# Turning q, k and the block mask by transposing DMAs in the later pairs of a fused attention and Fourier-MLP kernel

## The chip, the cores and the metric

The kernel runs on one core of one Trainium2 chip. The metric is the device time of one execution in microseconds (us), given as the median of several runs. TensorE (PE) multiplies matrices, VectorE (DVE), ScalarE (ACT) and GpSimd (POOL) work elementwise, and SyncE (SP) issues DMAs. PEld is TensorE's loading of weights, which overlaps the products.

## The reference, cut to what matters

Attention over q, k, v of shape (4 batches, 8 heads, 768 positions, 64), all float32. The keys form 12 blocks of 64. Each query may see its own block and the three blocks whose mean key has the largest product with it, below the diagonal:

```python
k_rep = k.reshape(B, H, n_blocks, block, D).mean(axis=3)
gate_scores = np.einsum('bhsd,bhnd->bhsn', q, k_rep)
gate_scores = np.where(causal, gate_scores, -1000000000.0)
top_idx = np.argsort(gate_scores, axis=-1)[..., -top_k:]
...
scores = scale * np.matmul(q, k.transpose(0, 1, 3, 2))
scores = np.where(mask, scores, -1000000000.0)
...
X = np.fft.fft(x, axis=1)
X = np.fft.fft(X, axis=2)
mixed = np.real(X).astype(np.float32)
u = x + mixed
un = (u - mu) / np.sqrt(var + 1e-06)
ch = np.maximum(un @ w_ch1, 0.0) @ w_ch2
return (u + ch).astype(np.float32)
```

Here x is the attention output of a batch, 768 positions by 512 (the heads side by side), and the MLP has 2048 hidden units.

## The kernel before, in words

Two heads of one batch form a pair; there are 16 pairs (0 to 15), four to a batch. For a pair, the main loop runs six steps of scores (`stage_S`: score products into `sc`, then one exponential on ACT into `ptl`) and, at fixed steps (`USUAL`), the rest of the work of this pair and of the two that follow:

- `load_qk`, `load_v`: q and k four pairs ahead, v two pairs ahead, on the sync queue, in float32 (`qn`, `kn`, `vn`).
- `stage_A`: TensorE transposes q and k (tile `tp`, twelve float32 transposes a pair). VectorE sums the keys of each block out of it (`kr`, L294). The turned k goes to `kI` in float16 (ACT, L313), the turned q to `qT`, and from there by POOL to `qg` (`cast_q`, L242).
- `stage_B`: the gate. Up to pair 7 it is a float32 product of `qT` with the block sums `kr24`. From pair 8 on (`SPLIT = 8`), q and the sums are each written as a high and a low float16 part (`qh`, `ql`, `krx`; L289, L290, L306, L307), and the product has 48 columns. VectorE takes the third largest (`mx`, L342) and writes a 0/1 mask `gmp`.
- `stage_C`: TensorE transposes the mask (`gt`, L356) and VectorE copies it into rows 64 to 75 of `qg` (L359). Those rows of `kI` hold -60000 at each block's own number, so the score product adds the mask.
- `stage_AV`: the product with v (`av`, L414). POOL casts v to float16 (`cast_v`, L237). Then the division and `fold`, which adds and subtracts halves for the Fourier transform; some small parts of it run on POOL (L443).

When a batch's four pairs are done, `queue_batch` puts its Fourier transform (`stage_S1`: `za`, `ya`; `stage_S2`: `mx`), its normalization (`stage_N`), the turning of the normalized x (`stage_T`: `unT`, by transposing DMAs for batches 1 and 2 and two parts of batch 3, L570) and its MLP (`stage_M1`: `ha`, `hb`; `stage_M2`: `ch`) into a feed. `filler` takes from the feed between the steps of the next pairs, by estimated costs and gaps, so that MLP products of the batch before stand between the score products. Batch 0's transform, in pairs 4 to 6, has no MLP work beside it.

The order on PE and POOL is the order of the program's text. On the other engines and the sync queue a scheduler chooses it. The MLP weights are loaded and cast to float16 by DMAs of POOL, each burst after a one-element copy that waits for a tile of a later pair (`pool_after`).

Of the kernel before, what the change touches and what calls it, by code (L numbers as in the profile page):

```python
# [19 lines left out]
def _consts_np():  # L20
    S = 768
    DM = 512
    NB = 12
    s = np.arange(S)

    sh = np.arange(S // 2)
    kk = 2 * np.arange(S // 4 + 1)[None, :] + np.arange(2)[:, None]
    arg = 2.0 * np.pi * ((sh[:, None, None] * kk[None]) % S) / S
    CS = np.cos(arg).astype(np.float16)
    SS = np.sin(arg).astype(np.float16)  # L30


    d = np.arange(DM // 4)
    l = 2 * np.arange(DM // 2)[None, :] + np.arange(2)[:, None]
    argd = 2.0 * np.pi * ((d[:, None, None] * l[None]) % DM) / DM
    CD = np.cos(argd).astype(np.float16)
    sn = np.sin(argd)
    sn[0] = np.sin(np.pi * l / 2)
    SDN, SDP = (-sn).astype(np.float16), sn.astype(np.float16)
    SDN[0, 0] = SDP[0, 0] = np.where(np.arange(DM // 2) % 2 == 0, 1.0, -1.0)  # L40
    ident32 = np.eye(128, dtype=np.float32)
    ident16 = np.eye(128, dtype=np.float16)
    jj = np.arange(128)
    ltri = np.where(jj[:, None] > jj[None, :], np.float32(NEG), 0.0).astype(np.float16)
    ut01 = (jj[:, None] <= jj[None, :]).astype(np.float16)
    nn = np.arange(NB)
    cz = np.where((s // 64)[:, None] >= nn[None, :], 0.0, -1e9).astype(np.float32)
    cz24 = np.concatenate([cz, cz], axis=1)
    oth01 = ((s // 64)[:, None] != nn[None, :]).astype(np.float16)
    oth24 = np.concatenate([oth01, oth01], axis=1)  # L50
    IndN = np.where(nn[:, None] == (s[None, :] // 64), NEG, 0.0).astype(np.float16)
    return dict(CS=CS, SS=SS, CD=CD, SDN=SDN, SDP=SDP, ident32=ident32, ident16=ident16,
                ut01=ut01, ltri=ltri, cz24=cz24, oth24=oth24, IndN=IndN)
# [65 lines left out]
def kernel(  # L119
# [65 lines left out]
    kI_t = [[const([128, S], F16, f"kI_{e}_{sl}") for sl in range(3)] for e in range(2)]  # L185
    v16_t = [const([128, 2, NST, 66], F16, f"v16_{sl}") for sl in range(4)]
    qg_t = [[const([128, S], F16, f"qg_{e}_{sl}") for sl in range(3)] for e in range(2)]
    warm = const([128, 512], F16, "warm")
    kr24_t = [const([128, 2 * NB], FP, f"kr24_{sl}") for sl in range(2)]
    krx_t = [const([128, 2, 2 * NB], F16, f"krx_{sl}") for sl in range(2)]  # L190
# [11 lines left out]
    SPLIT = 8  # L202
# [32 lines left out]
    def cast_v(kk):  # L235
        P[kk]["v16"] = v16_t[kk % 4]
        nc.gpsimd.tensor_copy(out=v16_t[kk % 4][:, :, :, 0:64], in_=P[kk]["vn"])  # L237

    def cast_q(kk):
        d = P[kk]  # L240
        for e in range(2):
            nc.gpsimd.tensor_copy(out=d["qg"][e][0:64, :],  # L242
                                  in_=d["qt" if kk < SPLIT else "qh"][64 * e:64 * e + 64, :])

# [21 lines left out]
    def stage_A(kk, who, g):  # L266
        d = P[kk]
        src = d["qn"] if who == 0 else d["kn"]
        if who == 0 and g == 0:
            d["qt"] = apool.tile([128, S], FP, tag="qT32", name=f"qT32_{kk}")  # L270
            if kk >= SPLIT:
                parts = d["qt"].bitcast(F16)
                d["qh"], d["ql"] = parts[:, 0:S], parts[:, S:2 * S]
            d["qg"] = [qg_t[e][kk % 3] for e in range(2)]
        if who == 1 and g == 0:
            d["kI"] = [kI_t[e][kk % 3] for e in range(2)]
            d["kr12"] = spool.tile([128, NB], FP, tag="kr12", name=f"kr12_{kk}", bufs=2)
            d["kr24"] = kr24_t[kk % 2]
        ps = pst([128, 3, 128], f"tp_{kk}_{who}_{g}")
        for i in range(3):  # L280
            nc.tensor.transpose(ps[:, i, :],  # L281
                                src[:, 3 * g + i, :, :].rearrange("p h d -> p (h d)"), id32)
        flat = ps.rearrange("p a c -> p (a c)")
        cols = slice(384 * g, 384 * (g + 1))
        if who == 0:
            if kk < SPLIT:
                (nc.scalar.copy if kk == LATE else nc.vector.tensor_copy)(out=d["qt"][:, cols], in_=flat)
            else:
                nc.scalar.activation(out=d["qh"][:, cols], in_=flat, func=AF.Copy, scale=QS)  # L289
                STT(out=d["ql"][:, cols], in0=flat, scalar=QS, in1=d["qh"][:, cols], op0=MULT, op1=SUB)  # L290
            if g == 1 and kk != LATE:
                cast_q(kk)
        else:
            nc.vector.tensor_reduce(out=d["kr12"][:, 6 * g:6 * g + 6],  # L294
                                    in_=ps.rearrange("p a (x c) -> p a x c", x=2),
                                    axis=mybir.AxisListType.X, op=ADD)
            if g == 1 and kk < SPLIT:
                for e in range(2):
                    nc.vector.tensor_copy(out=d["kr24"][64 * e:64 * e + 64, NB * e:NB * (e + 1)],
                                          in_=d["kr12"][64 * e:64 * e + 64, :])  # L300
            elif g == 1:
                d["krx"] = krx_t[kk % 2]
                for e in range(2):
                    r, c = slice(64 * e, 64 * e + 64), slice(NB * e, NB * (e + 1))
                    hi, lo = d["krx"][r, 0, c], d["krx"][r, 1, c]
                    nc.vector.tensor_scalar(out=hi, in0=d["kr12"][r, :], scalar1=QS, scalar2=None, op0=MULT)  # L306
                    STT(out=lo, in0=d["kr12"][r, :], scalar=QS, in1=hi, op0=MULT, op1=SUB)  # L307
            for e in range(2):
                dst, src_ = d["kI"][e][0:64, cols], flat[64 * e:64 * e + 64]
                if kk < EARLY and g == 1 and e == 1:  # L310
                    nc.vector.tensor_copy(out=dst, in_=src_)
                else:
                    nc.scalar.copy(out=dst, in_=src_)  # L313

# [3 lines left out]
    def stage_B(kk):  # L318
# [9 lines left out]
        else:  # L328
            gps = pst([128, NG, 2, 2 * NB], f"g_{kk}")
            krx = d["krx"].rearrange("p o n -> p (o n)")  # L330
            for st in range(1, NST):
                for n, part in enumerate((d["qh"], d["ql"])):
                    nc.tensor.matmul(gps[:, st - 1, :, :].rearrange("p o n -> p (o n)"),
                                     part[:, 128 * st:128 * (st + 1)], krx, start=(n == 0), stop=(n == 1))
            nc.vector.tensor_tensor(out=gsf, in0=gps[:, :, 0, :], in1=cz24[:, 1:NST, :], op=ADD)
            nc.vector.tensor_tensor(out=gsf, in0=gps[:, :, 1, :], in1=gsf, op=ADD)
# [12 lines left out]
        else:  # L349
            STT(out=gm, in0=gm, scalar=QS, in1=oth24[:, 1:NST, :, :], op0=MULT, op1=MULT)  # L350

    def stage_C(kk):
# [5 lines left out]
        for e in range(2):  # L358
            nc.vector.tensor_copy(out=d["qg"][e][64:64 + NB, 128:S],  # L359
                                  in_=gt[32 * e:32 * e + NB].rearrange("p a c -> p (a c)"))  # L360
# [17 lines left out]
    def stage_S(kk, e, s):  # L378
        d = P[kk]
        if s == 0:  # L380
            d.setdefault("pt", {})[e] = apool.tile([128, 3 * SEC], F16, tag=f"ptl{e}",
                                                   name=f"ptl_{kk}_{e}")
# [3 lines left out]
        for (jt, a0, a1, co) in SECS[s]:  # L386
            diag = by_pe and a0 == 128 * jt
            nc.tensor.matmul(sp[:, co:co + (a1 - a0)],  # L388
                             d["kI"][e][0:76, 128 * jt:128 * (jt + 1)],
                             d["qg"][e][0:76, a0:a1], start=True, stop=not diag)  # L390
            if diag:
                nc.tensor.matmul(sp[:, co:co + 128], id16, ltri, start=False, stop=True)  # L392
        nc.scalar.activation(out=pt[:, SEC * s:SEC * (s + 1)], in_=sp[:, 0:SEC], func=AF.Exp,  # L393
                             scale=0.125 if kk < SPLIT else 0.125 / QS)
# [218 lines left out]
    def queue_batch(b, start):  # L613
# [7 lines left out]
        turn_gap = 1.0 if turns else t_gap  # L621
# [24 lines left out]
        units.append(Unit(arm, 0.0, last, 10.0 if turns == NST else 0.8))  # L646
# [32 lines left out]
    with tc.manual_schedule(engines={mybir.EngineType.PE, mybir.EngineType.Pool}):  # L679
# [12 lines left out]
        for t in krx_t:  # L692
            nc.gpsimd.memset(t, 0.0)
        for t in gmp_t:
            nc.vector.memset(t, 0.0)
        for sl in range(3):
            for e in range(2):
                nc.gpsimd.dma_start(kI_t[e][sl][64:64 + NB, :], dr["IndN"].ap())
        nc.gpsimd.dma_start(ut01, dr["ut01"].ap())
        for e in range(2):  # L700
            for sl in range(3):
                nc.gpsimd.memset(qg_t[e][sl][64:64 + NB, 0:128], 0.0)
        load_v(0)
        for sl in range(4):
# [43 lines left out]
        for kk in range(NK):  # L748
            at = NORM if kk == NORM_SLOT else USUAL
            for p in range(6):  # L750
# [9 lines left out]
                if p == 1 and kk - 1 == NORM_SLOT:  # L760
                    main(stage_B, 0.35, kk + 1)
                if p == at["A1"] and kk + 2 < NK:
                    main(stage_AA, 0.7, kk + 2, 1)
                if p == at["C"] and kk + 1 < NK:
# [7 lines left out]
                if p == at["A0"]:  # L772
                    if kk + 2 < NK:
                        main(stage_AA, 0.7, kk + 2, 0)
# [6 lines left out]
                if p == at["B"] and kk + 2 < NK:  # L781
                    main(stage_B, 1.05 if kk + 2 < SPLIT else 0.35, kk + 2)
# [5 lines left out]
            if kk in (2, 4):  # L788
                pool_after(P[kk + 2]["qt"])
                load_w1(kk // 2 - 1)  # L790
            if kk in (6, 7):
                pool_after(P[kk + 2]["qt" if kk + 2 < SPLIT else "ql"])
                load_w2(2 * kk - 12)
                load_w2(2 * kk - 11)
# [35 lines left out]
```

## Time and profile before

| what | us |
|---|---|
| median of three runs | 329.2 |
| the three runs | 328.54, 329.2, 331.66 |
| the profiled execution | 330.56 |
| its span, first to last instruction | 328.8 |
| granted TensorE clock, mean | 0.995 |

The groups that the change touches, from the page's groups by form (count, busy us, mean ns of one):

| group | count | busy us | mean ns |
|---|---|---|---|
| PE `tp` of q and of k, 128x128 float32 | 96 + 96 | 14.0 + 14.0 | 275 |
| PE `gt`, 128x128 | 80 | 7.3 | 222 |
| PE `g`, float32, 24 columns (pairs 0 to 7) | 80 | 9.9 | 265 |
| PE `g`, float16, 48 columns (pairs 8 to 15) | 80 | 3.3 | 183 |
| ACT `kI`, 64x384 | 57 | 27.0 | 474 |
| ACT `qT` (the high part), 128x384 | 16 | 7.0 | 489 |
| DVE `qT` (the low part), 128x384 | 16 | 8.1 | 544 |
| DVE `kr`, 128x384 to 128x6 | 32 | 17.0 | 549 |
| DVE `qg` from `gt`, 12x640 | 32 | 15.5 | 484 |
| POOL `qg` from the float16 `qT`, 64x768 | 16 | 14.0 | 872 |

The DMA engines were busy 44% of the span in all: q1 (sync queue) 34.5%, q0 (POOL's queue, most of it the MLP weights) 8.8%. A busy time counts from an instruction's start to its end, and products on TensorE overlap, so the sum of their means is more than the time they take; what a group takes is read from its start to the start of the next.

### The profile page before, as it was taken

Reading aid. Unit: us, or ns where it says so; the run is one execution under the profiler, and the core shown is the slowest. Engines: PE = TensorE matmul, PEld = TensorE weight load, DVE = VectorE, ACT = ScalarE, POOL = GpSimd, SP = SyncE. Lnnn points to the kernel's source line nnn. Section 1 sums busy time; section 2 is a strip of 40 time slices with the busy share of each in tenths; the row PEclk is TensorE's granted clock in tenths of the full one; section 3 lists DMA queues with packets and bytes.
Section 4 is the critical chain, followed back from the end, with each engine's and each line's share of the span. In section 5 each row is a group of like instructions: output and inputs, shape, how many; then the busy total and the mean of one; then the engine's idle time right before and its main releaser. Section 6 shows DMA issues by size and latency. Waiting matters only on the chain.

```text
span 328.8 us, 6922 instructions
## 1 busy us (share of the span) xinstructions
PE 309.1 (94%) x2656; PEld 199.5 (61%) x2656; DVE 229.8 (70%) x736; ACT 179.9 (55%) x276; POOL 84.3 (26%) x137
## 2 busy tenths in 40 slices
PE   7799998997799999998999999997999999999994
PEld 3577776976566667654666776553666654566442
DVE  3778879489786898998667889995357588433211
ACT  3178888598976766446595856345564302244000
POOL 8444573540464030505041131302030000000000
PEclk9999998899999999999999999999999999999999
DMA  8995989992499642434733000114100011200021
GB/s 201 244 260 135 268 129 227 155 208 50 98 181 202 114 98 50 140 85 114 190 76 74 0 2 35 45 53 96 66 0 2 0 67 70 90 3 0 34 96 64
DMA packets 92929, 33.02 MB, mean 100 GB/s; under 512 B 85352, under 2 KB 88752, under 8 KB 92896
## 3 DMA queue, kind: packets, MB, share of 16 engines
q1 hardware_dynamic: 87600, 27.71, 34.5%
q0 software_dynamic: 3552, 4.40, 8.8%
q10 hardware_dynamic: 1744, 0.46, 0.6%
q8 instruction: 21, 0.34, 0.4%
q14 instruction: 12, 0.10, 0.1%
HBM read 28.63 MB, written 6.29 MB: 106 GB/s over the span
## 4 chain that ended last, share of the span: by engine, by line
PE 68%; DVE 19%; ACT 7%; DMA 2%; issue 2%; ACTq 0%; DVEq 0%
PE ch L603 19%; PE ha L589 15%; PE hb L589 8%; PE sc L388 7%; PE av L414 4%; ACT ptl L393 3%; ACT kI L313 3%; PE g L325 3%; PE za L488 2%; PE tp L281 2%; DVE mx L342 2%; DVE kr L294 2%; DVE bst L528 2%; DVE ptl L399 2%; DVE u L526 2%
## 5 line engine op out<-in xcount | busy, mean ns | idle before, releaser
L393 ACT ACTIVATE ptl<-sc 128x896 f16<-128x896 f32 x96 | 87.3, 918 | 43.9 <-PE sc L388 34.4
L603 PE MATMUL ch<-w_sb,hT 128*128 128x512 f16 x384 | 91.2, 379 | 0.9 <-DVE qT L290 0.9
L589 PEld LDWEIGHTS <-w_sb 128*128 128x128 f16 x512 | 48.6, 97 | 37.7 <-issue 3.8
L589 PE MATMUL ha<-unT,w_sb 128*128 128x512 f16 x256 | 65.7, 379 | 0.6 <-DMA unT<-x 0.5
L603 PEld LDWEIGHTS <-hT 128*128 128x128 f16 x384 | 36.4, 97 | 36.3 <-issue 0.8
L388 PE MATMUL sc<-qg,kI 76*128 76x512 f16 (+3 forms) x256 | 55.0, 307 | 3.4 <-ACT ptl L393 3.4
L592 ACT ACTIVATE hT<-ha 128x512 f16<-128x512 f32 x64 | 38.1, 598 | 30.7 <-PE ha L589 30.5
L594 DVE TENSOR_SCALAR hT<-hb 128x256 f16<-128x256 f32 x64 | 26.7, 420 | 30.3 <-PE hb L589 30.2
L589 PE MATMUL hb<-unT,w_sb 128*128 128x256 f16 x256 | 38.4, 272 | 1.7 <-DMA unT<-x 1.6
L434 POOL TENSOR_TENSOR fs<-x 128x384 f16<-128x384 f16 x12 | 10.9, 909 | 106.7 <-DVE x L420 91.9
L388 PEld LDWEIGHTS <-kI 76*128 76x128 f16 x256 | 24.1, 100 | 19.5 <-issue 2.6
L313 ACT CAST kI<-tp 64x384 f16<-64x384 f32 x57 | 27.0, 474 | 14.6 <-DVE kr L294 13.5
L606 DVE TENSOR_TENSOR u<-ch,u 128x512 f32<-128x512 f32 x24 | 16.4, 683 | 19.6 <-PE ch L603 19.3
L414 PEld LDWEIGHTS <-ptl 128*128 128x128 f16 x672 | 24.1, 97 | 3.1 <-DVE ptl L399 0.4
L414 PE MATMUL av<-v,ptl 128*128 128x65 f16 x672 | 25.7, 193 | 0.1
L294 DVE TENSOR_REDUCE kr<-tp 128x6 f32<-128x384 f32 x32 | 17.0, 549 | 8.2 <-PE tp L281 8.0
L561 ACT ACTIVATE x<-u,nmr,rstd 128x512 f16<-128x512 f32 x12 | 8.9, 804 | 18.8 <-issue 17.0
L392 PE MATMUL sc<-ltri,id 128*128 128x128 f16 x84 | 18.6, 222 | 0.0
L420 DVE TENSOR_TENSOR x<-av,rcp 128x384 f16<-128x384 f32 x32 | 17.8, 556 | 1.0
L399 DVE TENSOR_TENSOR ptl<-ptl,ut 128x384 f16<-128x384 f16 x36 | 13.8, 419 | 5.7 <-ACT ptl L393 5.7
L528 DVE BATCH_NORM_STATS2 bst<-u 128x6 f32<-128x512 f32 x24 | 16.6, 692 | 1.2 <-ACT u L524 0.7
L359 DVE COPY qg<-gt 12x640 f16<-12x640 f16 x32 | 15.5, 484 | 2.0 <-PE gt L356 1.1
(115 smaller groups left out, 408.2 us busy)
## 6 DMA issues: line engine op xcount, KB each, us to landing
vn<-in_v_dram SPq DMA_DIRECT2D x32, 192.0 KB, 3.6
out_dram<-u SPq DMA_DIRECT2D x24, 256.0 KB, 2.0
kn<-in_k_dram SPq DMA_DIRECT2D x30, 192.0 KB, 3.4
qn<-in_q_dram SPq DMA_DIRECT2D x30, 192.0 KB, 3.3
w_sb<-in_moe_w_ch_dram POOLq DMA_DIRECT2D x8, 256.0 KB, 7.0
w_sb<-in_moe_w_ch_dram POOLq DMA_DIRECT2D x4, 512.0 KB, 8.8
cs_sb<-c_CS SPq DMA_DIRECT2D x1, 289.5 KB, 4.6
ss_sb<-c_SS SPq DMA_DIRECT2D x1, 289.5 KB, 4.8
```

What stands on the lines that cost most here:

```text
L294: nc.vector.tensor_reduce(out=d["kr12"][:, 6 * g:6 * g + 6], in_=ps.rearrange("p a (x c) -> p a x c", x=2), axis=mybir.AxisListType.X, op=ADD)
L313: nc.scalar.copy(out=dst, in_=src_)
L388: nc.tensor.matmul(sp[:, co:co + (a1 - a0)], d["kI"][e][0:76, 128 * jt:128 * (jt + 1)], d["qg"][e][0:76, a0:a1], start=True, stop=not diag)
L392: nc.tensor.matmul(sp[:, co:co + 128], id16, ltri, start=False, stop=True)
L393: nc.scalar.activation(out=pt[:, SEC * s:SEC * (s + 1)], in_=sp[:, 0:SEC], func=AF.Exp, scale=0.125 if kk < SPLIT else 0.125 / QS)
L399: nc.vector.tensor_tensor(out=dg, in0=dg, in1=um, op=MULT)
L414: nc.tensor.matmul(av[:, st, 0:65], pt[:, o:o + 128], d["v16"][:, e, jt, 0:65], start=(cnt == 0), stop=(cnt == 20))
L528: nc.vector.bn_stats(out=bst, in_=u_b[:, kt, :])
L589: nc.tensor.matmul(hp_, w1_sb[:, dt, 128 * it:128 * (it + 1)], unT[:, dt, c0:c1], start=(dt == 0), stop=(dt == NDT - 1))
L592: nc.scalar.activation(out=hT[:, c0:c1], in_=hp_, func=AF.Relu)
L594: nc.vector.tensor_scalar(out=hT[:, c0:c1], in0=hp_, scalar1=0.0, scalar2=None, op0=mybir.AluOpType.max)
L603: nc.tensor.matmul(cps, x["hT"][it][:, 128 * st:128 * (st + 1)], w2_sb[:, it, :], start=(it == 0), stop=(it == NIT - 1))
```

## The change

From pair 9 on, TensorE no longer turns q, k and the mask.

- `split` casts q and k, as they lie in memory, to float16 (ACT) into `qs` and `ks` and puts the rest of q beside it, in `qs`, and the rest of k into `klo` (DVE). The sync queue then turns `qs` into `qhl` (high and low parts of q in one tile) and `ks` into `kI`, each by one transposing DMA of twelve 128x128 blocks. `ks` has the block numbers of `IndT` in its columns 64 to 75, so they arrive in the rows where `kI` needs them. The block runs with an order edge: its instructions stand behind the last exponential issued so far on ACT and behind batch 0's normalization on DVE.
- `stage_R` gets the block sums from products of `ks` and `klo` with a two-column matrix of ones, 24 small products a pair.
- `stage_B` of such a pair comes one step into the pair before it, has ten products of 24 columns, and writes the mask into `qs`; a third transposing DMA turns that into `qg`. `stage_C` and `cast_q` have no work in these pairs.
- `SPLIT` is 9: pair 8 has the float32 gate.
- The sync queue keeps the order of the program's text.
- MLP weights follow pairs 1, 2 (w1) and 3, 4 (w2); before, pairs 2, 4 and 6, 7.
- `ptl` has one buffer per head, v three; `kI` and `qg` hold both heads in one tile. The gap before the turned x is 4.0 (was 1.0) and the one after it 7.0 (was 10.0).

The diff, cut:

```diff
-    SPLIT = 8
+    SPLIT = 9
...
+    def turn(dst, src):
+        nc.sync.dma_start_transpose(dst.rearrange("p s e c -> p (s e) c"),
+                                    src.rearrange("p s e c -> p (s e c)"))
+
+    def split(kk):
+        d = P[kk]
+        kn, qn = d["kn"], d["qn"]
+        d["qs"] = qs = qs_t[kk % 2]
+        d["qhl"] = apool.tile([128, S], FP, tag="qT32", name=f"qhl_{kk}").bitcast(F16).rearrange(
+            "p (s e c) -> p s e c", e=2, c=128)
+        khi, qhi = ks[:, :, :, 0:64], qs[:, :, :, 0:64]
+        nc.scalar.activation(out=qhi, in_=qn, func=AF.Copy, scale=QS)
+        STT(out=qs[:, 1:NST, :, 64:128], in0=qn[:, 1:NST, :, :], scalar=QS, in1=qhi[:, 1:NST, :, :],
+            op0=MULT, op1=SUB)
+        turn(d["qhl"], qs)
+        nc.scalar.activation(out=khi, in_=kn, func=AF.Copy, scale=QS)
+        turn(kI_t[kk % 3], ks)
+        STT(out=klo, in0=kn, scalar=QS, in1=khi, op0=MULT, op1=SUB)
+        d["kI"], d["qg"] = kI_t[kk % 3], qg_t[kk % 3]
+
+    def stage_R(kk):
+        d = P[kk]
+        d["krs"] = krs = krs_t[kk % 2]
+        rps = pst([64, 2, NB], f"r_{kk}")
+        for st in range(NST):
+            for e in range(2):
+                o = rps[:, e, 2 * st:2 * st + 2]
+                nc.tensor.matmul(o, ks[:, st, e, 0:64], ind2, start=True, stop=False)
+                nc.tensor.matmul(o, klo[:, st, e, :], ind2, start=False, stop=True)
+        hi, lo = krs[0:64, :, 0, :], krs[0:64, :, 1, :]
+        nc.vector.tensor_copy(out=hi, in_=rps)
+        nc.vector.tensor_tensor(out=lo, in0=rps, in1=hi, op=SUB)
+        nc.scalar.copy(out=krs[64:128, :, :, :], in_=krs[0:64, :, :, :])
...
-            STT(out=gm, in0=gm, scalar=QS, in1=oth24[:, 1:NST, :, :], op0=MULT, op1=MULT)
+            STT(out=d["qs"][:, 1:NST, :, 64:64 + NB], in0=gm,
+                scalar=QS * QS, in1=oth24[:, 1:NST, :, :], op0=MULT, op1=MULT)
+            turn(qg_t[kk % 3], d["qs"])
...
-        turn_gap = 1.0 if turns else t_gap
+        turn_gap = 4.0 if turns else t_gap
...
-        units.append(Unit(arm, 0.0, last, 10.0 if turns == NST else 0.8))
+        units.append(Unit(arm, 0.0, last, 7.0 if turns == NST else 0.8))
...
-    with tc.manual_schedule(engines={mybir.EngineType.PE, mybir.EngineType.Pool}):
+    with tc.manual_schedule(engines={mybir.EngineType.PE, mybir.EngineType.Pool, mybir.EngineType.SP}):
...
-                if p == 1 and kk - 1 == NORM_SLOT:
-                    main(stage_B, 0.35, kk + 1)
-                if p == at["A1"] and kk + 2 < NK:
+                if p == 1 and (kk - 1 == NORM_SLOT or SPLIT <= kk + 1 < NK):
+                    main(stage_B, 0.3 if kk + 1 >= SPLIT else 1.05, kk + 1)
+                if p == at["A1"] and kk + 2 < min(SPLIT, NK):
                     main(stage_AA, 0.7, kk + 2, 1)
...
                     if kk + 2 < NK:
-                        main(stage_AA, 0.7, kk + 2, 0)
+                        if kk + 2 < SPLIT:
+                            main(stage_AA, 0.7, kk + 2, 0)
+                        else:
+                            with tc.issue_after(P[kk]["exp"].ins), tc.issue_after(X[0]["normed"].ins):
+                                split(kk + 2)
...
-                    main(stage_B, 1.05 if kk + 2 < SPLIT else 0.35, kk + 2)
+                    if kk + 2 < SPLIT:
+                        main(stage_B, 1.05, kk + 2)
+                    else:
+                        main(stage_R, 0.6, kk + 2)
...
-            if kk in (2, 4):
+            if kk == 3:
+                nc.gpsimd.memset(ks[:, :, :, 64 + NB:128], 0.0)
+                for t in qs_t:
+                    nc.gpsimd.memset(t[:, 0, :, 64:128], 0.0)
+                for e in range(2):
+                    nc.sync.dma_start(ks[:, :, e, 64:64 + NB],
+                                      dr["IndT"].ap().rearrange("(st p) n -> p st n", p=128))
+                    nc.gpsimd.memset(ind2[:, e:e + 1], 0.0)
+                    nc.gpsimd.memset(ind2[64 * e:64 * e + 64, e:e + 1], 1.0)
+            if kk in (1, 2, 3, 4):
                 pool_after(P[kk + 2]["qt"])
-                load_w1(kk // 2 - 1)
-            if kk in (6, 7):
-                pool_after(P[kk + 2]["qt" if kk + 2 < SPLIT else "ql"])
-                load_w2(2 * kk - 12)
-                load_w2(2 * kk - 11)
+                if kk < 3:
+                    load_w1(kk - 1)
+                else:
+                    load_w2(2 * kk - 6)
+                    load_w2(2 * kk - 5)
```

## The prediction

> **What bounds the kernel now.** I read the page's busy shares first, then the busy times by stretch, then the order of TensorE's work, then the waits, then the queues.
>
> ```profile
> PE 309.1 (94%) x2656; PEld 199.5 (61%) x2656; DVE 229.8 (70%) x736; ACT 179.9 (55%) x276; POOL 84.3 (26%) x137
> ```
>
> By stretch (length, then busy time of PE, PEld, DVE, ACT, POOL, clock, DMA share, GB/s):
>
> ```profile
> 18.60:50.20 31.60, 29.58 (x373) 23.74 (x372) 25.43 (x95) 26.79 (x36) 17.15 (x26) 1.00 0.90 193
> 50.20:88.70 38.50, 33.99 (x390) 27.23 (x388) 30.54 (x112) 32.00 (x51) 12.85 (x20) 0.96 0.72 147
> 125.90:249.70 123.80, 120.01 (x1031) 74.44 (x1028) 95.44 (x298) 72.92 (x111) 26.75 (x33) 1.00 0.26 68
> 249.70:325.50 75.80, 74.69 (x446) 40.73 (x443) 37.09 (x84) 16.74 (x28) 0.80 (x2) 1.00 0.12 43
> ```
>
> From 125.9 us (pair 9) on TensorE has 120.0 of 123.8 us, 17.7 us a pair: what it is spared there is time, what other engines are spared is not. Up to 50 us the DMA engines are at 0.90, and between 50 and 89 us TensorE is idle 4.5 us in the chain of batch 0, which has no MLP work beside it. The pieces that the change touches, on TensorE's timeline (start, length, what):
>
> ```profile
> 132.40 0.82 PE L281 MATMUL tp<-id,qn 128*128 128x128 f32 x6
> 133.05 0.27 PE L515 MATMUL mx<-cd_sb,yT 128*128 128x256 f16 x1
> ...
> 135.69 0.46 PE L356 MATMUL gt<-id,gmp 128*44 128x128 f16 x5
> 136.08 0.28 PE L515 MATMUL mx<-cd_sb,yR 128*128 128x256 f16 x1
> ...
> 141.83 0.41 PE L333 MATMUL g<-krx,qT 128*128 128x48 f16 x10
> 142.08 0.27 PE L515 MATMUL mx<-cd_sb,yR 128*128 128x256 f16 x1
> ```
>
> Matmuls overlap, so a group costs from its start to the next group's start: six tp 0.65 us, five gt 0.39 us, ten g 0.25 us. TensorE's waits after 125.9 us:
>
> ```profile
> PE hb L589 <- DMA unT<-x: 1.6, 1, 1.6
> PE ch L603 <- DVE qT L290: 0.9, 1, 0.9
> PE mx L515 <- DVE u L606: 0.8, 1, 0.8
> ```
>
> The sync queue's timeline, with six transposing DMAs of four 128x128 blocks each, and with loads beside half of w1 (issued by POOL at 41.78):
>
> ```profile
> 150.25 7.85 SPq L570 DMA_TRANSPOSE unT<-x  x6
> 158.19 1.12 SPq L224 DMA_DIRECT2D qn<-in_q_dram  x2
> ```
>
> ```profile
> 42.96 0.96 SPq L224 DMA_DIRECT2D kn<-in_k_dram  x2
> 45.27 5.60 SPq L224 DMA_DIRECT2D qn<-in_q_dram  x2
> ```
>
> And POOL around batch 0's transform:
>
> ```profile
> 50.02 0.83 POOL L237 CAST v<-vn 128x768 f16<-128x768 f32 x1
> 55.08 0.59 POOL L443 TENSOR_TENSOR ft<-fs 128x6 f16<-128x6 f16 x1 [4.23 <-DVE fs L435]
> 55.62 0.53 POOL L443 TENSOR_TENSOR xmid<-fs 128x6 f16<-128x6 f16 x1
> ```
>
> **Part 1, TensorE of pairs 9 to 15.** Each loses twelve tp (2 x 0.65) and five gt (0.39, and a 0.09 gap ahead of them: four ch of 0.216 from 134.74 end at 135.60): 1.78 us. It gains the 24 products of stage_R, each a load of 64 columns and two moving columns. No row has that shape. Below, the ten g set the pace, 0.025 us each; above, the gt, 0.39/5 = 0.078. So 0.60 to 1.87 us; I take 0.030, 0.72 us, nearest to g, because gt streams 128 columns and stage_R two. The g keep their number and halve their columns: nothing. Net 1.06 us a pair, 7.4 us in seven pairs (8.3 gain to 0.6 loss). Pair 8 goes back to the float32 gate: ten passes, 1.09 us in the early pairs (32.57 to 33.66), for 0.25: 0.8 us lost. Sum: **-6.6**.
>
> **Part 2, VectorE and ScalarE.** VectorE loses per pair two kr (0.55), four small krx (0.16), two qT (0.54) and two qg copies (0.48), 3.8 us; it gains two splits over 640 and 768 elements, by L290's 0.54 for 384 some 0.9 and 1.1, and two small copies, 0.3. ScalarE loses four kI (0.47) and two qT (0.49), 2.9 us, and gains two casts of 128x768 (0.84, the f16 copy of that size in L469) and a small copy, 1.9. Neither bounds the stretch (95 and 73 of 124 us), so this is worth only a wait: the 0.9 us of ch on qT, whose instruction goes. **-0.9**. The casts sit behind the third exponential of a pair and ahead of the fourth; that costs nothing while the fourth score product comes later than the 1.7 us of casts, and MLP products stand between (ACT waited 31.8 us for sc in this stretch). Without that cover it would be up to 1.7 us a pair. POOL loses two qg casts of 0.87, which nobody awaited.
>
> **Part 3, the sync queue.** A turn is now twelve blocks. The rows give 7.85/6 = 1.3 us of queue for four, landing 2.4 us after issue. Bounds for twelve: 1.3 (one instruction, whatever its size) and 7.2 (three landings in a row); I take three times 1.22, 3.7 us, since 24 blocks one after another ran at 0.33 us a block. Three turns, 11.0; six loads at 0.4 to 0.5, 2.7; one or two results, 0.5: 14.2 of 16.6 us a pair. It fits with 2.4 to spare. In program order a pair's queue reads: load v, turn mask of the next pair, turn q, turn k, load k and q. The mask turn waits for VectorE's mask, some 5 us after the gate at 4.5 us: it lands near 14.5 us and is needed at 16.6. The q turn lands near 18 and the next gate asks at 21; the k turn near 22, and the single ks buffer is written again near 24. All are covered, by 2 to 3 us each.
>
> The cover goes where batch 1's six norm turns (7.85) stand ahead of pair 11's mask turn, in pair 10. Their x is ready about 5 us after the last mx (u 0.68, bst 0.69, aggregate 0.18, ten steps of 0.2, x 0.54, another u 0.68); queue 7.85 + 3.7, landing 1.2 more: 17.8 us after that mx, while the next score product comes one pair, 16.6 us, after it. **+1.0** (0 to 2.7 where x comes as late as before, 7 us). In batch 2 the norm turns stand behind three large turns but meet a quieter VectorE; the 2.1 us that ha and hb wait there stay: 0 (-2.1 to +1.5).
>
> [...]
>
> **Part 4, weights early.** Four bursts (two halves of w1, two of w2) follow pairs 1 to 4, not 2, 4, 6 and 7, into DMA engines that are at 0.90 already. Beside the first burst of before, two loads held the sync queue 5.60 us where they take 1.12 elsewhere, and the longest k or q load landed after 9.8 us, median 3.5: 6.3 late. Loads of q and k run two pairs ahead and hide this. v does not: POOL casts it in order, and behind that cast now stand seven memsets (about 1.4, by the rows of 0.74 for 128x768 and 0.12 to 0.2 for small ones), two w2 issues (0.78 each), and only then ft and xmid, which the transform of batch 0 awaits. POOL had 4.23 us to spare there; 3.1 are used. A v late by 0 to 6.3 costs 0 to 5.2 us with no MLP work to fill it; I take 2.5, the middle, as the burst is moved but not yet seen beside this load. **+2.5**. What w2 leaves at 91 to 112 us frees no time: TensorE was busy 36.6 of 37.2 us there.
>
> One probability buffer fewer, three v slots, the new layout of kI and qg and the IndT load cost nothing: the last reader of each buffer (the AV product) ends two steps of a pair before its next writer.
>
> **Sum.** -6.6 - 0.9 + 1.0 + 2.5 = -4.0. The profiled execution took 330.56 us (span 328.8, 1.8 around it) and would take 326.6; the median of the runs, 329.2, lies 1.4 lower: **325.2 us**.
>
> **Rivals.**
> (a) The early loads stay hidden; the slack of before speaks for it, the DMA share of 0.90 against: 322.7 us.
> (b) The small products pace at 0.050, half way to gt: 1.20 us a pair, gain 0.58 x 7, and 3.4 us less than forecast: 328.6, no change. [...] Against: av paces at 0.03 (27.29 to 27.93 for 21).
> (c) Slower: the turns fill the sync queue. It decides from (16.6 - 3.2)/3 = 4.5 us a turn on. At 5.0 a pair lasts 18.2 us, 1.6 x 7 = 11 more: 336 us. For it: a landing takes 2.4 for four blocks, and loads share the queue. Against: six turns in a row kept 1.3 us each.
> (d) A block costs its own full landing: twelve times 2.4/4 is the 7.2 above, 24.8 us a pair, +57 us: 382. 24 blocks in 7.85 us speak against it. [...]
> That the turns do not happen is no rival: 84 tp and 35 gt are gone from the program's order.
>
> **Chances.** Forecast 0.45, (a) 0.15, (b) 0.15, (c) 0.19, (d) 0.02, early loads worse than 5 us 0.04. A measurement of this kernel tells about 1%, 3.3 us, from no change. The forecast's 325.2 is just beyond that bound (325.9), with its own range 321 to 329: 0.31 of its 0.45 is faster, 0.14 the same. With (a): faster 0.46; with (b): same 0.29; slower 0.25. The range takes in (a) and its larger gain and reaches to (c): 320 to 336.
>
> **What would show it.** Right: PE's busy time in pairs 9 to 15 falls by some 7 us, r products start every 0.03 us, turns hold the queue 3.7 us, sc waits once on qg in pair 11 for about 1 us, and za of batch 0 starts 2 to 3 us later than 56.6. Wrong: sc or g waiting for turns in every pair (c), r at 0.05 or more (b), za on time (a), or waits of exponentials on casts.

## The result: 1.4% slower, and the profile after

The changed kernel takes 334.29 us (median of four runs, 333.69 to 335.19), the kernel before beside it 329.63 (four runs, 328.54 to 331.66). The ratio is 1.0143, with a 95% interval of 1.0101 to 1.0184. The profiled execution has a span of 331.9 us, 3.1 more than before. The forecast was 325.2, faster; the time lies in its range of 320 to 336, on the wrong side. Here and below, a run more than 1.5% above the fastest of its kernel is left out of a ratio.

The page's busy shares, in the form of the line before:

```profile
PE 307.5 (93%) x2705; PEld 196.9 (59%) x2705; DVE 219.5 (66%) x691; ACT 172.1 (52%) x253; POOL 71.2 (21%) x126
```

Every engine has less to do, and the kernel is slower: something waits. The same stretches as before (length, then busy time of PE, PEld, DVE, ACT, POOL, clock, DMA share, GB/s) say where:

```profile
...
50.20:88.70 38.50, 29.25 (x320) 23.70 (x319) 27.17 (x96) 24.91 (x38) 17.65 (x34) 0.86 1.11 186
...
125.90:249.70 123.80, 119.99 (x1139) 74.11 (x1137) 90.59 (x289) 70.50 (x100) 17.31 (x23) 1.00 0.69 139
```

Between 50 and 89 us PE is busy 29.3 us where it was 34.0, the granted clock is 0.86 where it was 0.96, and the DMA share stands at 1.11 (it sums the times of packets, so it can pass 1). From 125.9 us on PE is as full as before.

The start of each pair (its first exponential on ACT) cuts the span into a ledger. Four kernels stand in it, two of them experiments told below:

| stretch, us | before | changed | bursts late | fold on VectorE |
|---|---|---|---|---|
| start to pair 4 | 50.25 | 50.65 | 50.81 | 50.53 |
| pair 4 | 15.13 | 22.36 | 13.48 | 16.02 |
| pairs 5 and 6 | 23.37 | 23.56 | 22.63 | 22.65 |
| pair 7 to the end | 240.01 | 235.35 | 235.33 | 235.31 |
| span | 328.8 | 331.9 | 322.2 | 324.5 |

From pair 7 on the change gains 4.7 us, the same within 0.04 us in three kernels that have it. Pair 4, batch 0's Fourier transform, loses 7.2. The profiles of the two experiments are the fastest of their runs, 2.2 and 2.0 us below the medians, so the ledger shows them at their best. POOL's timeline of the changed kernel there (start, length, what, idle time ahead of it and what ended that):

```profile
48.67 0.82 POOL L245 CAST v<-vn 128x768 f16<-128x768 f32 x1 [7.46 <-DMA vn<-in_v_dram]
...
49.56 2.17 POOL L264 DMA_DIRECT2D w_sb<-in_moe_w_ch_dram  x4
...
59.64 0.82 POOL L245 CAST v<-vn 128x768 f16<-128x768 f32 x1 [4.03 <-DMA vn<-in_v_dram]
60.40 0.62 POOL L829 MEMSET ks<- 128x624 f16 x1
...
61.88 1.55 POOL L269 DMA_DIRECT2D w_sb<-in_moe_w_ch_dram  x2
63.44 0.23 POOL L475 TENSOR_TENSOR ft<-fs 128x6 f16<-128x6 f16 x1
```

Before, that v cast came at 50.02 and ft at 55.08. Now ft comes at 63.44, behind the late cast (0.8 us), the memsets and the small copy (1.5) and two issues of w2 (1.6). TensorE waits for it, first the kernel before, then the changed one:

```profile
56.57 2.14 PE L488 MATMUL za<-ss_sb,ft 128*128 128x193 f16 x12
```

```profile
58.66 0.69 PE L520 MATMUL za<-ss_sb,ft 128*128 128x193 f16 x3
63.73 1.64 PE L520 MATMUL za<-ss_sb,ft 128*128 128x193 f16 x9 [4.38 <-POOL ft L475]
...
67.11 1.22 PE L446 MATMUL av<-v,ptl 128*128 128x65 f16 x21
68.16 0.41 PE L520 MATMUL za<-ss_sb,ft 128*128 128x193 f16 x3
```

In the changed kernel the three za at the first line take 0.69 us and the last three 0.41, and 21 av take 1.22 where others take 0.80: the clock is at half. The stretches of the changed kernel show it (the eighth number is the granted clock):

```profile
50.60:57.80 7.20, 4.38 (x53) 3.19 (x53) 6.99 (x22) 4.89 (x8) 4.88 (x9) 1.00 0.99 165
57.80:63.70 5.90, 1.55 (x8) 0.78 (x7) 2.18 (x5) 3.01 (x5) 3.88 (x13) 0.50 1.01 185
63.70:68.10 4.40, 4.37 (x41) 4.13 (x42) 1.05 (x2) 0.76 (x2) 1.82 (x4) 0.51 1.26 157
```

So the wait has a second price: the 4.4 us after it run at half speed, some 2 us. The clock records give one unbroken half-speed stretch of 10.24 us, 57.8 to 68.0; before, it was 3.41 us (55.9 to 59.3). The clock thus fell before the long wait began (59.35) and stayed down behind it. The longer stretch is three times the shorter. Ahead of this fall PE was busy 4.38 of 7.2 us and never idle for more than 1.04 us at a time; why the clock fell there is not shown.

Why v comes late is on the sync queue, first of the changed kernel, then of the kernel with late bursts:

```profile
37.84 9.23 SPq L232 DMA_DIRECT2D kn<-in_k_dram  x2
...
48.60 1.62 SPq L240 DMA_DIRECT2D vn<-in_v_dram  x2
```

```profile
36.56 2.26 SPq L232 DMA_DIRECT2D kn<-in_k_dram  x2
...
40.65 2.54 SPq L240 DMA_DIRECT2D vn<-in_v_dram  x2
```

Beside the first burst (POOL, 34.21) two k loads hold the queue for 9.23 us instead of 2.26, so v of pair 5 is issued at 48.60 and not at 40.65. There it meets the second burst (49.56): its first half landed 4.4 us after its issue, its second 10.1. One burst moved the load into the next one.

### The profile page after: what moved, and what is told of

It reads as the page before. It is cut to its first block, busy times and chain, and to the rows that moved or that the text cites. A ratio compares the mean times of both kernels' runs of the same rounds, so it can differ in the third digit from the quotient of the medians.

```text
span 331.9 us, 7001 instructions
## 1 busy us (share of the span) xinstructions
PE 307.5 (93%) x2705; PEld 196.9 (59%) x2705; DVE 219.5 (66%) x691; ACT 172.1 (52%) x253; POOL 71.2 (21%) x126
## 4 chain that ended last, share of the span: by engine, by line
PE 74%; DVE 8%; DMA 8%; ACT 4%; POOL 2%; issue 1%; SPq 1%; ACTq 0%; DVEq 0%; POOLq 0%
PE ch L635 25%; PE ha L621 14%; PE sc L420 8%; PE hb L621 7%; PE av L446 5%; DMA vn<-in_v_dram 3%; PE g L354 2%; PE za L520 2%; ACT kI L307 2%; ACT ptl L425 2%; PE ya L524 2%; PE mx L547 2%; DMA qg<-qs 2%; PE mx L548 2%; DMA cz<-c_cz 1%; DVE mx L372 1%
## 5 line engine op out<-in xcount | busy, mean ns | idle before, releaser
L635 PE MATMUL ch<-w_sb,hT 128*128 128x512 f16 x384 | 89.8, 379 | 0.0
L635 PEld LDWEIGHTS <-hT 128*128 128x128 f16 x384 | 36.6, 97 | 37.5 <-issue 0.2
L245 POOL CAST v<-vn 128x768 f16<-128x768 f32 x16 | 13.8, 863 | 31.9 <-DMA vn<-in_v_dram 30.1
L307 ACT CAST kI<-tp 64x384 f16<-64x384 f32 x29 | 13.7, 474 | 8.9 <-DVE kr L295 7.9
L593 ACT ACTIVATE x<-u,nmr,rstd 128x512 f16<-128x512 f32 x12 | 8.9, 804 | 18.2 <-DVE nmr L586 18.1
L250 POOL CAST qg<-qT 64x768 f16<-64x768 f32 x18 | 14.8, 822 | 8.7 <-DVE qT L291 4.2
L431 DVE TENSOR_TENSOR ptl<-ptl,ut 128x384 f16<-128x384 f16 x36 | 13.0, 383 | 5.0 <-ACT ptl L425 5.0
```

The lines of the kernel that those rows point to most:

```text
L635: nc.tensor.matmul(cps, x["hT"][it][:, 128 * st:128 * (st + 1)], w2_sb[:, it, :], start=(it == 0), stop=(it == NIT - 1))
```

## The experiments

All times are medians; a ratio is to the kernel before on the same chip.

**1. The bursts back where they were.**

```diff
-            if kk in (1, 2, 3, 4):
-                pool_after(P[kk + 2]["qt"])
-                if kk < 3:
-                    load_w1(kk - 1)
-                else:
-                    load_w2(2 * kk - 6)
-                    load_w2(2 * kk - 5)
+            if kk in (2, 4):
+                pool_after(P[kk + 2]["qt"])
+                load_w1(kk // 2 - 1)
+            if kk in (6, 7):
+                pool_after(P[8]["qt"] if kk == 6 else P[9]["qs"][:, 0, 0, :])
+                load_w2(2 * kk - 12)
+                load_w2(2 * kk - 11)
```

> The changed kernel with its weight bursts put back behind pairs 2 and 4 (w1) and 6 and 7 (w2), nothing else. Theory (the early bursts starve the v loads of batch 0, POOL casts v late, and za of batch 0 waits behind that cast): pair 4 goes back from 22.4 to about 15 us and the late part keeps its 5.7 us gain, so 329.6 - 5.7 + 0 to 2 = 324 to 326 us, ratio to the kernel before 0.983 to 0.989, clock at half speed for one stretch of 3.4 us as before, and no za wait on POOL above 1 us. Rival 1 (the loss in pair 4 comes from something else of the change, such as the sync queue in program order): the time stays at 333 to 335 us. Rival 2 (the bursts only move the loss to pairs 6 to 8, where the sync queue now keeps program order): 327 to 331 us.

Measured: 326.26 us (324.03, 324.24, 328.28 and 328.52), ratio 0.9897 (0.9802 to 0.9991). In the profiled run, the fastest, pair 4 lasts 13.5 us, v of pair 5 is cast at 50.57 us, and no za wait is left:

```profile
56.81 1.16 PE L520 MATMUL za<-ss_sb,ft 128*128 128x193 f16 x12
```

The loss is the early bursts, and rival 1 falls. Pairs 6 to 8 are at most 0.1 us longer than in the changed kernel, so rival 2 falls in this run; the two runs at 328 lie in its range and have no profile, so what they lose stays open.

**2. The early bursts alone, in the kernel before** (the reverse edit).

> The kernel before with only its weight bursts moved behind pairs 1 to 4. Theory (the bursts alone carry the loss): 329.6 + 5 to 9 = 335 to 339 us, ratio 1.015 to 1.027, pair 4 near 20 to 22 us long, v cast in pair 4 late by 6 to 10 us. Rival (program order of the sync queue is needed for the loss, since there a late load holds up the v load behind it): 328 to 331 us, ratio within 1% of 1.

Measured: 331.32, 337.00, 337.45 and 338.33 us, median 337.22. They lie too far apart for a ratio: three are in the theory's range, and the lowest stands next to the rival's. In the profiled one (337.45) v of pair 5 is cast at 56.04, 6.0 us late, so v comes late under early bursts in the old kernel too. Pair 4 lasts 18.1 us there, but no quicker run has a profile; whether the bursts alone cost the old kernel time, and how much, stays open.

**3. The small fold operations on VectorE.** POOL's ft and xmid for batch 0's last pair move:

```diff
-tt((ft[0] if b == 0 else fo[1])[:, :, 0:1], f[:, :, 128:129], f[:, :, 384:385], SUB, nc.gpsimd)
+tt((ft[0] if b == 0 else fo[1])[:, :, 0:1], f[:, :, 128:129], f[:, :, 384:385], SUB,
+   nc.vector if b == 0 else nc.gpsimd)
...
-f[:, :, 384:385], ADD, nc.gpsimd)
+f[:, :, 384:385], ADD, nc.vector if b == 0 else nc.gpsimd)
```

> The changed kernel with the two small fold operations of batch 0's last pair (one ft, one xmid, 128x6) on VectorE in place of POOL, so that za does not stand behind POOL's late cast of v. Theory (the loss is POOL's order, not the late v itself): the 4.4 us that za waits on ft vanish and with them most of the half-speed clock stretch (10.2 to 3.4 us): 334.3 - 5 to -7 = 327 to 329 us. Rival 1 (the next AV product needs the late v anyway): PE waits for v16 in its place, 332 to 335 us. Rival 2 (VectorE is too loaded there): -2 to -3, 331 to 332.

Measured: 328.31 us (ten runs), ratio 0.9967 (0.9930 to 1.0005). Its POOL and TensorE:

```profile
60.62 0.82 POOL L245 CAST v<-vn 128x768 f16<-128x768 f32 x1 [6.42 <-DMA vn<-in_v_dram]
```

```profile
57.64 2.12 PE L521 MATMUL za<-ss_sb,ft 128*128 128x193 f16 x12
```

v is as late as in the changed kernel, even 1 us later, and za starts at 57.64. The late v hurts only because the fold stands behind its cast on POOL. Both ways of breaking the chain, a punctual v or another engine for the fold, give back 6 us and more.

**4. Filling the wait.** Ahead of batch 0's transform: `stage_W(20)`, products into a tile that nothing reads.

> The changed kernel with 20 products of 512 columns, whose result nothing reads, put ahead of batch 0's transform, where PE stands idle for 4.4 us. Theory (the idle time has a second price, since the granted clock falls to half for 10.2 us behind it): PE is kept busy through the wait, the half-speed stretch behind it is gone or down to 3.4 us, and the time falls by 1.5 to 3 us to 331.5 to 333 us, the wait itself staying. Rival (the half-speed clock costs nothing there, since PE waits anyway for what follows): 334 to 336 us.

Measured: 332.64 us (332.11 to 334.17, four runs), ratio 1.0105 (1.0033 to 1.0178). That is in the theory's range, but the interval takes in the changed kernel's 1.0143, and pair 4 stays at 22.4 us:

```profile
57.81 0.58 PE L420 MATMUL sc<-qg,kI 76*128 76x512 f16 x1 [0.48 <-ACT ptl L425]
...
58.73 6.73 PE L399 MATMUL warm<-warm 128*128 128x512 f16 x20
```

```profile
61.27 0.82 POOL L245 CAST v<-vn 128x768 f16<-128x768 f32 x1 [5.60 <-DMA vn<-in_v_dram]
...
65.08 0.24 POOL L475 TENSOR_TENSOR ft<-fs 128x6 f16<-128x6 f16 x1
```

The score product ahead of the fill already takes 0.58 us for 0.39: the clock fell at 56.4, before the long wait, after a stretch in which PE was idle a third of the time (busy 4.04 of 6.10 us). The fill brought it back: half speed ended at 63.3, after 6.8 us in place of 10.24, and the 12 za, 12 ya and 21 av behind the wait took 2.65 us (65.29 to 67.94), where the changed kernel took 4.43 for three za fewer (63.73 to 68.16). That is the second price, some 2 us. But v was cast 1.6 us later in this run, and with it ft came at 65.08 for 63.44, which took the gain in pair 4. The profile's 1.6 us less is 0.9 in pair 6, where the second half-speed stretch (88.5 to 91.9 in the changed kernel) is gone, and small amounts elsewhere.

**5. One burst held back until v has landed.** The second half of w1 waits for v of pair 5:

```diff
                     load_v(kk + 2)
+                    if kk == 3:
+                        pool_after(P[5]["vn"][:, 1, 0, :])
+                        load_w1(1)
```

> The changed kernel with one burst held back by some microseconds: the second half of w1 waits until v of pair 5 has landed, so that in the trace it comes just behind that load and not 0.2 us behind the issue of it; the other three bursts stay early. Theory (the loss is one collision: the second head of v(5), issued at 49.39 us, stands beside the burst of 49.56 us and lands after 10.1 us where the first head took 4.4): v(5) lands near 53 us, its cast comes before 56 us, za is on time, pair 4 lasts 15 to 17 us in place of 22.4, and the time is 327 to 330 us. Rival (any early burst delays the fold of batch 0, since POOL waits and issues ahead of it): 332 to 335 us, the wait of za moved or put down to another load.

Measured: 335.52 us, ratio 1.0176 (1.0134 to 1.0217): a miss, and the rival is right. v landed at 53.48, 4.9 us after its issue, as expected. But POOL now stood waiting for it:

```profile
53.54 0.18 POOL L254 COPY dummyp<-vn 1x1 f32<-1x1 f32 x1 [4.84 <-DMA vn<-in_v_dram]
53.77 2.16 POOL L264 DMA_DIRECT2D w_sb<-in_moe_w_ch_dram  x4
...
61.11 0.82 POOL L245 CAST v<-vn 128x768 f16<-128x768 f32 x1
...
64.91 0.23 POOL L475 TENSOR_TENSOR ft<-fs 128x6 f16<-128x6 f16 x1
```

From 53.5 to 65 us POOL has no idle time: issues, fold, q casts, v cast, memsets, issues, and at their end ft, 1.5 us later than in the changed kernel. The mend put a wait of 4.84 us and the issues ahead of the fold and of v's cast, and so traded one delay for another. The cause is not the collision of two transfers alone, but POOL's order: whatever holds POOL up in these 15 us holds up za.

**6. The sync queue's order left to the scheduler**, as before (`EngineType.SP` taken out of `manual_schedule`).

> The changed kernel with the sync queue's order left to the scheduler, as before; nothing else. Theory (program order is not what loses the time; the bursts are): pair 4 stays above 18 us, and the time lies within 2% of 334.3 us, 328 to 338. Rival 1 (program order is the loss, since loads of q and k stand ahead of the v load in it): pair 4 falls to 15 to 16 us and the time to 326 to 328 us. Rival 2 (program order is what makes three turns a pair fit): waits for qg or qhl in every pair from 11 on, above 340 us.

Measured: 337.08 us (335.76 to 341.20, four runs), ratio 1.0223 (1.0177 to 1.0269). Pair 4 lasts 23.2 us, so program order is not what loses the time there. From pair 7 on it lasts 238.6 us, 3.3 more than the changed kernel: 2.3 us in one wait of sc for qg, and a half-speed stretch in pair 14. Neither rival holds. Program order may help a little, but the interval touches that of the changed kernel (1.0101 to 1.0184).

**7. Both mends: late bursts, and the fold on VectorE.**

> The changed kernel with late weight bursts and with batch 0's two small fold operations on VectorE: the two mends together. Theory (each takes away the same wait of za): no more than late bursts alone, 324 to 326 us, ratio 0.982 to 0.990. Rival (they add up, as the other fold helps where the burst after pair 4 slows the loads of pairs 5 and 6): 321 to 323 us.

Measured: **325.05 us** (323.98 to 326.74, six runs), ratio 0.9869 (0.9833 to 0.9905). They do not add up, as the theory had it. It beats the kernel before by 1.3% and the changed kernel by more.

**8. The same, with the gap behind the turned x at 10.0.**

> As the run before, and the gap behind the turned x is 10.0 again as in the kernel before, where the change has 7.0. Theory (hb and ha of batch 2 wait 2.1 us for the last turned x, and more filler work ahead of them covers it): those two waits vanish, 1 to 2 us less than the run before. Rival (the other batches lose as much, since their products come later and the last batch has more left): 0 to 2 us more.

Measured: 330.66 us (twelve runs), ratio 1.0025 (0.9994 to 1.0056): 5.6 us worse than the run before, a miss. The rival's direction is right, its 0 to 2 us too small. In its profile pair 15 lasts 19.9 us to its last exponential in place of 14.5, and pair 14 1.1 less. The two waits for the turned x are gone, but pair 15's mask turn stands in the sync queue behind batch 2's six norm turns, and the score product waits for it:

```profile
216.29 7.75 SPq L603 DMA_TRANSPOSE unT<-x  x6
224.13 1.46 SPq L310 DMA_TRANSPOSE qg<-qs  x1
```

```profile
227.97 0.91 PE L420 MATMUL sc<-qg,kI 76*128 76x512 f16 x3 [4.64 <-DMA qg<-qs]
```

From 227.0 to 233.8 the clock is at half, 5.9 us of products that by estimate cost 2.9 us more. In run 7 TensorE had stood in the two waits (2.0 us) while the turn landed: 4.6 - 2.0 + 2.9 is 5.5 us.

**9 and 10. Filling the short waits ahead of za**, with late bursts (9) and with late bursts and the fold on VectorE (10). The six products' result is read by nothing:

```diff
+                if kk == 4 and p in (3, 4):
+                    stage_W(3)
                 main(stage_S, 0.39, kk, p // 3, p % 3)
```

> The changed kernel with late weight bursts (as in the first experiment) and with three products of 512 columns, whose result nothing reads, ahead of the fourth and of the fifth score product of pair 4, where PE waits 0.8 us each time for an exponential. Theory (the granted clock falls to half at 56 to 58 us because PE is idle in 54 to 57 us, not because of the long wait of za behind it, which is why 20 products put ahead of za came too late): no half-speed stretch between 55 and 62 us, pair 4 at 13.5 to 14 us in every run, and the runs gather near the fast ones of the first experiment, 323.5 to 325 us. Rival (the clock falls for another reason, such as the load of the first 50 us): a stretch of 3.4 us stays in some or all runs, 325 to 328 us.

> The same six products in the kernel with late bursts and with batch 0's two small fold operations on VectorE (325.05 us without them). Theory: its half-speed stretch of 57.5 to 60.9 us goes and pair 4 falls from 16.2 to 14 us: 322.5 to 324 us, ratio to the kernel before 0.978 to 0.984. Rival: the stretch stays or moves behind, 325 us as before.

Measured: 325.64 us (323.68 to 327.48, seven runs) and 325.34 (324.01 to 325.64, six runs), ratios 0.9902 (0.9865 to 0.9939) and 0.9882 (0.9860 to 0.9905). Both medians are the rivals': the theories had 323.5 to 325 and 322.5 to 324. Run 9 shows nothing of the fill by its profile, since the profile of run 1 had no half-speed stretch in pair 4 either (13.5 us, with the fill 14.7). In run 10 the stretch goes. Without the fill (7) and with it (10):

```profile
50.50:57.50 7.00, 4.92 (x57) 3.37 (x55) 6.79 (x24) 5.57 (x9) 1.94 (x8) 1.00 0.90 155
57.50:61.00 3.50, 3.37 (x22) 3.15 (x23) 2.72 (x8) 2.33 (x4) 2.15 (x4) 0.51 1.07 232
```

```profile
51.50:57.50 6.00, 5.28 (x58) 3.55 (x57) 5.79 (x26) 5.17 (x8) 1.76 (x8) 1.00 0.78 146
57.50:61.00 3.50, 3.50 (x55) 3.25 (x54) 2.53 (x6) 3.21 (x7) 1.90 (x4) 1.00 1.04 201
```

PE busy 5.3 of 6.0 us ahead of the transform keeps the clock where 4.9 of 7.0 lost it, and pair 4 falls from 16.2 to 14.1 us. In this pair of profiles that part of the theory holds. Busy time alone does not settle when the clock falls: in run 7 PE was busy 1.82 of the 3.4 us from 224.8 on, and the clock stayed up. The medians do not move: half-speed stretches of 3.4 us stand elsewhere (18 to 22 us in run 10's profile, 81 to 84 and 224 to 228 in run 9's). Across the seven runs of 9, those at a mean clock of 0.995 and above took 323.7 and 323.9 us, the others 325.3 to 327.5. What decides in which run another stretch falls stays open.

**11. Every turn issued twice.**

```diff
-        nc.sync.dma_start_transpose(...)
+        for _ in range(2):
+            nc.sync.dma_start_transpose(...)
```

> The changed kernel with every transposing DMA of q, k and mask issued twice in a row, so that a turn holds the sync queue about 3 us and not 1.5. Theory (the sync queue has room for turns of up to 4.5 us, as forecast, and late loads are covered): the late part, from pair 8 to the end, keeps its length of 216.5 us within 2, the time is 333 to 337 us. Rival (the forecast had the landing wrong, and turns are on the path from two landings of 4 to 6 us on): 4 to 6 us in each of the seven pairs from 9 on, 355 us and more.

Measured: 378.59 us, ratio 1.1508 (1.1472 to 1.1544). The edit did not make turns of 3 us, since the second waits until the first, which writes the same tile, has landed (the sync queue's waits for these landings are 49.4 us in 21 turns):

```profile
159.30 5.55 SPq L311 DMA_TRANSPOSE kI<-ks  x2
```

At 5.5 us of queue a turn the pairs from 9 to 14 last 20 to 32 us. That is rival (c) of the prediction, above its threshold of 4.5, and dearer than its 11 us; half-speed stretches between 156 and 280 us, 37.5 us in all, have their part in it.

**12. Only w1 early, w2 as before.**

> The changed kernel with only w1 early (behind pairs 1 and 2) and w2 late (behind pairs 6 and 7). Theory (most of the wait of za is v(5) landing late beside w1's second half; the two issues of w2 that stand ahead of ft on POOL add their own 1.5 us, and the bursts of w2 disturb pairs 5 to 7 little): pair 4 falls from 22.4 to 20 to 21 us, the time from 334.3 to 332 to 333 us. Rival 1 (the w2 issues and their bursts carry most): 327 to 329 us. Rival 2 (they cost nothing): 334 us.

Measured: 333.31 us (332.96 to 335.30, four runs), ratio 1.0101 (1.0041 to 1.0160). The theory's 20 to 21 us for pair 4 is a miss, and rival 1 falls; it lasts 22.7 us: the w2 issues are gone from ahead of ft, but v was cast at 61.31 us, and ft came at 63.45 as in the changed kernel. The gain of 1 us in the median is no more than the spread of the runs. w1 alone carries the loss; the 1.5 us of the issues did not show, since v was cast 1.7 us later than in the changed kernel.

**13. A spare turn of two blocks behind every turn**, into a tile that nothing reads:

```diff
+        scr.append(scr.pop(0))
+        nc.sync.dma_start_transpose(scr[0].rearrange("p s e c -> p (s e) c"),
+                                    src[:, 0:1, :, :].rearrange("p s e c -> p (s e c)"))
```

> The changed kernel with a spare transposing DMA of two 128x128 blocks behind every turn of q, k and mask, into a tile that nothing reads; unlike the doubled turn it does not wait for the landing of the one ahead. It adds about 1.2 us of queue a turn, 1.5 to 2.7 us, still under the 3.7 us that were forecast. Theory (the queue has room for that, the doubled turns lost their 44 us since each held the queue 5.4 us): the part from pair 8 to the end stays within 2 us of 216.5, the time at 333 to 337 us. Rival (there is no room beyond what the turns take, so the forecast was saved by turns that are shorter than it took): 3 to 10 us more in pairs 9 to 14, 338 to 345 us.

Measured: 339.61 us, ratio 1.0281 (1.0242 to 1.0320): the rival. Its sync queue:

```profile
142.21 1.45 SPq L311 DMA_TRANSPOSE qg<-qs  x1
143.71 1.55 SPq L314 DMA_TRANSPOSE scr<-qs  x1
```

A turn and its spare hold 3.0 us. Pairs 10 and 11, where batch 1's six norm turns stand in the queue, last 3.1 and 2.1 us more; pairs 9 and 12 to 15 stay within 0.1, pair 8 within 0.4. Of these 5.2 us a half-speed stretch (170.1 to 176.9) has its part. Another 2.5 us fell in pair 4, so these 339.6 are not the turns' alone.

## Why the prediction was wrong, point by point

**Part 4, the early weights, is the step that failed: +2.5, bounds 0 to 5.2; measured +7.2 in pair 4.** The mechanism was named with its place: v late, POOL's cast in order, behind it memsets, two w2 issues, then ft and xmid, no MLP work to fill. The size was wrong in two ways. v was taken to be at most 6.3 us late, the longest delay seen beside one burst. Its cast came 9.6 us late, since two bursts followed each other: the first held the k loads, and so pushed the v load behind them into the second. And the wait was priced at its length, though the trace of before showed a half-speed stretch at that very place. Of the 7.2 us, 5.8 are idle time of TensorE in pair 4 (7.2 for 1.4), and 1.4 are products that take longer (busy 15.15 for 13.77), as half speed lasts 10.24 us and not 3.41. Against the profile with late bursts, which has no half-speed stretch there, the term is 8.9 us (22.36 against 13.48); by the medians it is 8.0 (334.29 against 326.26). The forecast's own "za starts 2 to 3 us later than 56.6" was the test: the bulk of them came at 63.73.

**Part 1 was right, and a little too high.** The 24 small products and the gap ahead of them take 0.85 us where 0.72 was forecast, one every 0.03 us:

```profile
163.32 0.17 PE L337 MATMUL r<-ind,ks 128*64 128x2 f16 x1
163.35 0.17 PE L338 MATMUL r<-ind,klo 128*64 128x2 f16 x1
```

By 1.78 - 0.85 = 0.93 us a pair, seven pairs give 6.5. Pair 8's float32 gate shows in pair 7, 18.83 us for 17.84: 1.0 for the forecast 0.8. That is -5.5 for -6.6. Rival (b), products at 0.05 us, falls.

**Part 2 was right.** The 0.9 us wait of ch on qT is gone, and in the late part TensorE waits nowhere for the new casts.

**Part 3 came out near its sum by luck, as two errors cancel.** sc waits once for qg, 0.7 us, in pair 11, as forecast (1.0, though its own terms, 17.8 less 16.6, give 1.2); the 1.6 us wait of hb stays. But a turn holds the queue 1.5 us, not 3.7. Had it been 3.7, the price would not have been 1.0: the spare turns show 5.2 us in pairs 10 and 11 at 3.0, the clock's part in it included. The cover of 2 to 3 us a pair held; the one worked out for the norm turns was too generous. For batch 2 it was thin as well: the 4.6 us of experiment 8 came with turns of 1.5 us.

Parts 1 to 3 were to give -6.5, and from pair 7 to the end they gave -4.7. The measured terms come near: -5.5, -0.9 for ch, +0.7 for sc on qg, and two short waits that nobody forecast, av on hT (0.8) and hb on hT (0.3), less the 0.8 of mx on u, which is gone: -5.4. The other 0.7 us is not explained. Taking the wrong term out, the forecast for the change without early weights is rival (a)'s 322.7 us; the kernel that is so measured 326.3, its two lower runs 324.0 and 324.2, and with the fold moved 325.05.

**The rivals.** (a), early loads hidden, is refuted by the trace itself. (c) and (d) did not happen: twelve blocks took 1.5 us of queue where four took 1.22, so a turn's queue time was not priced by its blocks. Yet it was (c) that stretched the range to 336, so that 334.29 lies in it is luck. The rival that came was the last and smallest, early loads worse than 5 us, at a chance of 0.04: it was an upper end of a term and should have been a case of its own, with the clock in it.

## What to carry to other kernels

A transfer that is moved earlier must be followed past the load it meets: ask which queue that load holds up, what is issued behind it, and whether that lands in the next burst. An in-order engine that both waits for loads and feeds the critical chain turns every late load into a late chain; moving two operations of 0.2 us off it was worth 6 us here. And a wait of TensorE of some microseconds is priced with its echo where the clock is down: here the products behind it ran at half speed, some 2 us.

## What the runs showed of the hardware

- The queue time of a transposing DMA hardly depended on its size here: mostly 1.55 us for two 128x128 blocks (experiment 13, right behind a larger turn), 1.22 for four (median, before and changed), 1.3 to 2.6 for twelve (changed, median 1.49). The landing did: mostly 2.4 us after issue for four, 3.8 to 5.9 for twelve.
- Loads of the sync queue beside a w1 burst of POOL's DMAs landed up to 11.8 us after issue in the changed kernel and 9.8 in the kernel before, where the medians of the q, k and v loads are 4.4 to 4.8 and 3.3 to 3.6. The four DMAs of the burst itself landed 4.4 to 8.3 us after issue where the sync queue was nearly empty (before, 59.89 us), and 5.8 to 10.8 beside loads (changed, 49.56): both slowed each other down.
- The clock fell to half not only in a long wait (at 227.0 us in experiment 8, in the wait of 4.64 us), but where PE was busy 4.4 of 7.2 us with no wait above 1.04 us (changed, 50.6 to 57.8 us). The half-speed stretches told above lasted 3.41 us (before, from 55.9 us) or a multiple of it (6.8 in experiment 4, 10.24 in the changed kernel).
